# Loading the upper half of each w1 and w2 piece from ScalarE's queue

## The chip, the cores and the metric

The kernel runs on 1 core of one Trainium2 chip. The metric is the device time of one execution in microseconds (us); of several runs the median is given. Everything below about the hardware's behaviour is read from the profile of this kernel.

## The reference: what is computed

Two blocks, one after the other. The first is a delta-rule recurrence over 4 batches, 8 heads, 768 steps and 48 features a head; the second is a feed-forward block without a nonlinearity on the 3072 x 384 result.

```python
def _attn_ref(q, k, v, beta):                    # (4, 8, 768, 48)
    k_n = k / (np.linalg.norm(k, axis=-1, keepdims=True) + 1e-06)
    state = np.zeros((B, H, D, D), dtype=np.float32)
    for t in range(S):
        kt, vt, bt = (k_n[:, :, t], v[:, :, t], beta[:, :, t, None])
        y[:, :, t] = np.einsum('bhd,bhde->bhe', q[:, :, t], state)
        v_old = np.einsum('bhde,bhd->bhe', state, kt)
        state = state + bt[:, :, :, None] * np.einsum('bhd,bhe->bhde', kt, vt - v_old)
    return y

def _moe_ref(x, w1, w2, w3, w_out):              # x 3072x384, w1 w2 384x1024,
    a = x @ w1                                   # w3 1024x1024, w_out 1024x384
    b = x @ w2
    h = a * b @ w3
    return (h @ w_out).astype(np.float32)
```

q, k, v and beta come as 32-bit floats. The four weights come as 64-bit floats: a division by a numpy square root makes them so.

## The kernel before, in words

**The recurrence in chunks.** The 768 steps are cut into 12 chunks of 64. For each chunk the kernel makes score matrices of the keys (`scores`, L359), inverts the unit triangular matrices on VectorE, two chunks at a time and 32 x 32 blocks at a time (`inverse`, L422; its two long lines are L442 and L449), goes through DRAM to bring the blocks into another layout (`to_blocks` L410 writes Ud, L428 reads Ub, L457 writes Vd, `from_blocks` L463 reads TT and T), completes the inverse with small matmuls (`corner`, L480; products L502, copies L518 and L529), and carries the state along (`chain`, L547, matmuls L555). `outputs` (L623, matmuls L656) writes the chunk's result transposed into xT: eight ScalarE copies (L677), then six small DMAs inside SBUF (L688).

**The feed-forward block.** w3 and w_out are multiplied beforehand (`fold`, L768, matmuls L771 and copies L778, after the transposes L762 and copies L765 of w3), since nothing stands between them. Then, for every two chunks, `ab` (L784) makes (x w1) and (x w2): three matmuls over the 384 rows for each block of 128 columns (L791), a ScalarE copy of the first product (L803), and a VectorE multiplication by the second (L807). GpSimd makes sums of these slabs (L860) and `o` (L865, matmuls L888) and `result` (L915) the output.

**The 64-bit weights.** A weight is loaded as pairs of 32-bit words and converted in the kernel. `load_pair` (L701) loads one piece into one of three `raw` buffers in turn, 1 MB each; `convert` (L711) makes half of a piece: two ScalarE operations (L717, L720), a shift on VectorE (L722), a sum on GpSimd (L724). There are 18 pieces: 4 of w_out, 8 of w3, 3 of w1 and 3 of w2. A piece of w_out or w3 is one DMA over 128 partitions. A piece of w1 or w2 (`load_w12`, L741) is 128 rows of the weight in the order in which xT holds the features, and takes four DMAs: 48 rows to partitions 0 to 47, 16 rows to 48 to 63, 48 rows to 64 to 111, 16 rows to 112 to 127. Each row is 8 KB. The last two are called the upper half here. w_out's converted pieces lie in the buffer of w2, so w2's conversion waits until the folds have read them.

**The order.** No scheduler chooses the order: `ORDER` (L39) is a list of step names, and each name advances one generator by one step. P names are loads of pieces (P12 to P17 those of w1 and w2, in the order P13, P12, P14, P15, P17, P16), C names conversions, k, q, v and p the loads of keys, queries and values, a and b the steps of `ab`. `in_text_order` (L161) then fixes the order on each engine as written, so every engine works through its own list strictly in order. SyncE (SP) issues nearly all DMAs; ScalarE issues only those of the first chunk of k and q (`act.dma_start` at L980 and L991). An instruction that issues a DMA first waits for its buffer (here: until GpSimd's L724 has read the piece three back) and for its semaphore: the DMAs share eight of these, called lanes below, and the lane's last DMA must have landed. A waiting DMA instruction holds up what stands behind it in its engine's list.

Of the kernel before, what the change touches and what calls it, by code (L numbers as in the profile page):

```python
# [90 lines left out]
def kernel(  # L91
# [15 lines left out]
    C = 64  # L107
# [32 lines left out]
    def in_turn(pool, shape, tag, n, name, dt=FP32):  # L140

        i = turns.get(tag, -1)
        while True:
            i = turns[tag] = (i + 1) % n
            if (tag, i) not in held:
                return pool.tile(shape, dt, tag=f"{tag}{i}", name=name, bufs=1)
# [14 lines left out]
    def in_text_order():  # L161
# [7 lines left out]
    pe, dve, act, pool, sync = nc.tensor, nc.vector, nc.scalar, nc.gpsimd, nc.sync  # L169
# [7 lines left out]
        out=strict[:], in_=strict[:], pattern=[[1, P]], compare_op=ALU.is_gt,  # L177
# [523 lines left out]
    def load_pair(i, n, srcs):  # L701

        raw = raws[i] = in_turn(ffn, [P, 2, CW, 2], "raw", 3, "raw", U32)
        for rows, src in srcs:
            to = raw[rows, :, 0:n].rearrange("p b n w -> p b (n w)")
            if n == CW:
                to = to.rearrange("p b n -> p (b n)")
            sync.dma_start(out=to, in_=src)
        yield

    def convert(i, hf, n, dst):  # L711
# [21 lines left out]
    def load_wo(j):  # L733
        src = moe_w_out[2 * j * P : (2 * j + 2) * P, :].bitcast(U32)
        return load_pair(j, DM, [(slice(0, P), src.rearrange("(b p) n -> p b n", b=2))])

    def load_w3(jc):
        src = moe_w3[jc * P : (jc + 1) * P, :].bitcast(U32)
        return load_pair(KF // 2 + jc, CW, [(slice(0, P), src)])

    def load_w12(i, src, m):  # L741
        srcs = []
        for e in range(2):
            a, b = D * (NP * e + m), D * (NP * e + NP - 1) + 16 * m
            srcs.append((slice(C * e, C * e + D), src[a : a + D, :].bitcast(U32)))
            srcs.append((slice(C * e + D, C * e + C), src[b : b + 16, :].bitcast(U32)))
        return load_pair(i, CW, srcs)
# [317 lines left out]
```

## Time and profile before

| | |
|---|---|
| median of 3 runs | 602.34 us (601.66 to 604.63) |
| the profiled execution | 601.93 us |
| its span in the profile | 600.2 us |
| mean granted TensorE clock | 0.98 |
| busy: PE, DVE, ACT, POOL | 90%, 55%, 27%, 29% |
| chain that ended last, PE's share | 80% |
| DMA queue of SP | 54.52 MB, 46.4% of 16 engines |
| DMA queue of ACT | 0.79 MB, 0.9% |
| queue of instructions | 1.08 MB, 0.8% |

How to read it: PE is TensorE's matmuls and PEld its weight loads, DVE is VectorE, ACT ScalarE, POOL GpSimd, SP SyncE; a q behind the name (SPq, ACTq) is the engine's sequencer, which issues DMAs and isn't counted as busy. A row of a timeline has the start in us, the length in us, engine, line, operation, tile written and tiles read with their shapes, a count, and in brackets how long the engine had been idle and what ended that. "issue" there means that the engine waited for nothing that the profile shows. A row of the chain of waits has start, length, and what the time went to. The times of a DMA are its issue; how long it took to land is given by the view of its tile.

The six pieces in question, from SP's timeline and the landings (us):

| load | issued | landed |
|---|---|---|
| 1: P13, w1 m=1 | 74.07 to 75.39 | 78.9 to 82.6 |
| 2: P12, w1 m=0 | 93.86 to 96.30 | 100.1 to 104.1 |
| 3: P14, w1 m=2 | 96.82 to 98.16 | 107.4 to 110.6 |
| 4: P15, w2 m=0 | 118.12 to 120.54 | 123.9 to 127.8 |
| 5: P17, w2 m=2 | 127.95 to 130.90 | 133.5 to 137.0 |
| 6: P16, w2 m=1 | 140.01 to 141.51 | 145.0 to 148.9 |

### The profile page before, as it was taken

The page shows a single profiled execution, that of the slowest core. Times are in us where ns is not written, and L with a number is a line of the kernel's source. Part 1 is how long each engine was busy: PE and PEld are TensorE (multiplying, and loading weights), DVE is VectorE, ACT ScalarE, POOL GpSimd, SP SyncE. Part 2 cuts the span into 40 slices and gives each one's busy share as a digit, 9 for nine tenths or more (in the row PEclk, how much of TensorE's full clock was granted, in tenths as well). Part 3 has the DMA queues.
Part 4 walks back from the last instruction along what each step waited for, and adds up shares of the span by engine and source line. Part 5 has one row for each costly group of instructions (what it writes and reads, how often), then busy time and mean ns, then how long its engine had stood idle before and what let it go on. Part 6 is the DMA issues. An engine that isn't in the chain of part 4 may idle for free.

```text
span 600.2 us, 19394 instructions
## 1 busy us (share of the span) xinstructions
PE 542.4 (90%) x8444; PEld 378.7 (63%) x8444; DVE 329.7 (55%) x788; ACT 164.2 (27%) x345; POOL 173.6 (29%) x222
## 2 busy tenths in 40 slices
PE   2378994889899999999999899999999999999997
PEld 2364663658678884558854569645588446884477
DVE  2457763457786379665696644975545963211012
ACT  3486653734312211131211312012310111320100
POOL 6364433230535700207203016021071001500051
PEclk9988996899999999999999989999999999999999
DMA  8959887596953356525546352463253021010001
GB/s 225 219 135 276 233 163 128 82 176 96 164 80 55 56 123 108 98 42 84 103 78 127 50 81 73 82 114 65 40 86 94 14 59 32 5 54 13 1 0 53
DMA packets 204404, 56.54 MB, mean 94 GB/s; under 512 B 193344, under 2 KB 199488, under 8 KB 202528
## 3 DMA queue, kind: packets, MB, share of 16 engines
q1 hardware_dynamic: 200128, 54.52, 46.4%
q10 hardware_dynamic: 4192, 0.79, 0.9%
q8 instruction: 66, 1.08, 0.8%
q14 instruction: 18, 0.15, 0.1%
HBM read 43.09 MB, written 11.01 MB: 90 GB/s over the span
## 4 chain that ended last, share of the span: by engine, by line
PE 80%; DMA 6%; issue 4%; DVE 4%; ACT 4%; SPq 1%; POOL 0%; ACTq 0%; DVEq 0%
PE ps_f L791 39%; PE ps_f L888 18%; PE ps_w L555 5%; PE ps_f L771 5%; PE ps_w L656 4%; DMA raw<-in_moe_w_dram 3%; PE ps_w L502 3%; PE ps_w L369 2%; PE ps_w L375 2%; DMA ktok<-in_k_dram 2%; DVE ps_w L449 1%; DVE tb L442 1%; DMA Vd<-Vb 1%; ACT raw L720 1%; PE ps_w L888 1%
## 5 line engine op out<-in xcount | busy, mean ns | idle before, releaser
L791 PE MATMUL ps_f<-xT,w2s 128*128 128x512 f32 (+1 forms) x336 | 134.2, 544 | 3.0 <-POOL w2s L724 2.8
L860 POOL TENSOR_TENSOR ab<-ab 128x256 f32<-128x256 f32 x96 | 66.8, 728 | 223.5 <-DVE ab L807 190.0
L791 PE MATMUL ps_f<-xT,w1s 128*128 128x512 f32 (+1 forms) x336 | 128.2, 532 | 0.3 <-issue 0.3
L791 PEld LDWEIGHTS ps_f<-xT,w2s 128*128 128x128 f32 x336 | 62.5, 191 | 57.9 <-issue 50.9
L791 PEld LDWEIGHTS ps_f<-xT,w1s 128*128 128x128 f32 x336 | 63.3, 190 | 55.8 <-issue 51.7
L803 ACT COPY ab<-ps_f 128x512 f32<-128x512 f32 (+1 forms) x56 | 27.9, 527 | 185.6 <-PE ps_f L791 185.6
L888 PE MATMUL ps_f<-w,ab 128*128 128x192 f32 x376 | 66.3, 330 | 0.0
L807 DVE TENSOR_TENSOR ab<-ab,ps_f 128x512 f32<-128x512 f32 (+1 forms) x56 | 32.9, 604 | 59.1 <-PE ps_f L791 58.5
L888 PEld LDWEIGHTS ps_f<-w,ab 128*128 128x128 f32 x376 | 61.2, 190 | 3.9 <-issue 2.7
L442 DVE TENSOR_TENSOR tb<-Vb,Ub 128x31 f32<-128x31 f32 (+15 forms) x124 | 43.9, 354 | 16.4 <-DMA Ub<-Ud 13.0
L771 PE MATMUL ps_f<-w2s,w3T 128*128 128x384 f32 x128 | 45.4, 507 | 4.9 <-ACT w3T L765 3.5
L888 PE MATMUL ps_f<-room,ab 128*128 128x192 f32 x272 | 48.0, 330 | 0.8 <-DVE room L919 0.8
L449 DVE TENSOR_TENSOR Vb<-Vb,tb 128x31 f32<-128x31 f32 (+15 forms) x124 | 44.6, 360 | 4.3
L888 PEld LDWEIGHTS ps_f<-room,ab 128*128 128x128 f32 x272 | 44.1, 190 | 1.6 <-issue 1.1
L677 ACT COPY xT<-ps_w 48x256 f32<-48x256 f32 x96 | 30.5, 366 | 49.1 <-PE ps_w L656 48.6
L272 POOL TENSOR_TENSOR sq<-ktok 128x384 f32<-128x384 f32 x24 | 20.2, 852 | 75.7 <-DVE tb L442 39.1
L381 DVE TENSOR_TENSOR U<-ps_w,wt 128x512 f32<-128x512 f32 x24 | 16.5, 689 | 42.6 <-PE ps_w L375 42.5
L771 PEld LDWEIGHTS ps_f<-w2s,w3T 128*128 128x128 f32 x128 | 24.2, 195 | 21.5 <-ACT w3T L765 4.0
L375 PE MATMUL ps_w<-KQ 48*64 48x64 f32 x768 | 29.4, 227 | 6.3 <-issue 4.7
L724 POOL TENSOR_TENSOR w<-w,raw 128x512 uint32<-128x512 uint32 x16 | 20.7, 1298 | 33.1 <-DVE w L722 15.7
L375 PEld LDWEIGHTS ps_w<-KQ 48*64 48x64 f32 x768 | 26.1, 140 | 5.6 <-issue 3.9
L541 POOL TENSOR_TENSOR vtok<-vtok,n 128x384 f32<-128x384 f32 x24 | 19.8, 838 | 33.3 <-DMA vtok<-in_v_dram 33.3
(104 smaller groups left out, 644.7 us busy)
## 6 DMA issues: line engine op xcount, KB each, us to landing
raw<-in_moe_w_dram SPq DMA_DIRECT2D x8, 1024.0 KB, 8.1
vtok<-in_v_dram SPq DMA_DIRECT2D x24, 192.0 KB, 4.5
raw<-in_moe_w_dram SPq DMA_DIRECT2D x12, 384.0 KB, 6.7
out_dram<-osb SPq DMA_DIRECT2D x46, 96.0 KB, 2.7
ktok<-in_k_dram SPq DMA_DIRECT2D x44, 96.0 KB, 3.5
raw<-in_moe_w_out_dram SPq DMA_DIRECT2D x4, 768.0 KB, 5.0
Ud<-U SPq DMA_DIRECT2D x48, 64.0 KB, 2.3
Ub<-Ud SPq DMA_DIRECT2D x6, 512.0 KB, 3.9
```

The lines of the kernel that those rows point to most:

```text
L375: pe.matmul(ps[half(z ^ j), 1, n + C * j : n + C * j + C], lhsT=x[:, 0, :], rhs=x[:, j, :], start=True, stop=True,)
L442: dve.tensor_tensor(out=tv, in0=V[:, 0 : s + 1, s : s + 1].to_broadcast([P, s + 1, n]), in1=U[:, s, s + 1 : BS].unsqueeze(1).to_broadcast( ...
L449: dve.tensor_tensor(out=o, in0=o, in1=tv, op=ALU.subtract)
L555: pe.matmul(out(ps, r, h, z), lhsT=lhs(r, h, z), rhs=rhs(r, h, z), start=True, stop=True,)
L656: i = pe.matmul(region(h, z, r), lhsT=lhs, rhs=rhs, start=part[n] not in part[:n], stop=part[n] not in part[n + 1 :],)
L677: act.copy(out=xT[f, p:NP:2, b : b + NR, cc, :].rearrange("p a r t -> p r a t"), in_=pyv[f, z, b : b + NR],)
L771: pe.matmul(ps[:, 0:DM], lhsT=w3Ts[jc, kc // 4][:, kc % 4 * P : kc % 4 * P + P], rhs=wo[:, kc], start=(kc == 0), stop=(kc == KF - 1),)
L791: pe.matmul(ps[:].rearrange("p b c t -> p b (c t)"), lhsT=w[:, m, js], rhs=x[:, m, :, c0:c1].rearrange("p b c t -> p b (c t)"), start=(m = ...
L803: act.copy(out=t, in_=ps)
L807: dve.tensor_tensor(out=t, in0=t, in1=ps, op=ALU.mult)
L860: pool.tensor_tensor(out=o_, in0=x_, in1=y_, op=op)
L888: pe.matmul(ps[b][:, b, :], lhsT=abs_[u, HF * f + i][:, t0 : t0 + P], rhs=ws_[w][:, i], start=first and i == 0 and (b == 0 or n == "F"), s ...
```

## The change

In `load_pair` the DMA of a row range that begins at partition 64 or above (C is 64) is issued by ScalarE, every other one by SyncE as before. Only `load_w12` hands over such ranges, two of four for each piece, so 12 DMAs of 3 MB in all move. The buffers, the bytes, the converted results and ORDER stay as they are; in ScalarE's list a moved DMA stands where its step stands in ORDER. The lanes are dealt out anew, so that some DMAs of SP now share a lane with one of ScalarE, and the reverse.

```diff
         raw = raws[i] = in_turn(ffn, [P, 2, CW, 2], "raw", 3, "raw", U32)
         for rows, src in srcs:
+            dma = act.dma_start if rows.start >= C else sync.dma_start
             to = raw[rows, :, 0:n].rearrange("p b n w -> p b (n w)")
             if n == CW:
                 to = to.rearrange("p b n -> p (b n)")
-            sync.dma_start(out=to, in_=src)
+            dma(out=to, in_=src)
         yield
```

The function that hands over the ranges:

```python
def load_w12(i, src, m):
    srcs = []
    for e in range(2):
        a, b = D * (NP * e + m), D * (NP * e + NP - 1) + 16 * m
        srcs.append((slice(C * e, C * e + D), src[a : a + D, :].bitcast(U32)))
        srcs.append((slice(C * e + D, C * e + C), src[b : b + 16, :].bitcast(U32)))
    return load_pair(i, CW, srcs)
```

## The prediction

> **What bounds the kernel now.** I read the page first, then the chain of work that ended last, then PE's waits and its timeline, and at the places found there the timelines of SP and ACT and the DMA view. From the page:
>
> ```profile
> PE 542.4 (90%) x8444; PEld 378.7 (63%) x8444; DVE 329.7 (55%) x788; ACT 164.2 (27%) x345; POOL 173.6 (29%) x222
> ...
> q8 instruction: 66, 1.08, 0.8%
> ...
> raw<-in_moe_w_dram SPq DMA_DIRECT2D x12, 384.0 KB, 6.7
> ```
>
> PE is busy for 90% of the span. The windows put its idle time early: between 220 and 600 us it idles 9.8 of 380 us, between 75 and 180 us it idles 18.8 of 105. The six loads that the change touches are issued at 74.07, 93.86 (two), 118.12, 127.95 and 140.01 us, all in that early part, so only what reaches PE before about 180 us counts; behind that PE passes on whatever delay or lead it has. PE's timeline there:
>
> ```profile
> 96.28 0.47 PE L375 MATMUL ps_w<-KQ 48*64 48x64 f32 x2 [2.19 <-issue]
> ...
> 105.59 0.33 PE L502 MATMUL ps_w<-T,U 33*33 33x32 f32 x4 [6.15 <-issue]
> ...
> 113.21 0.91 PE L771 MATMUL ps_f<-w2s,w3T 128*128 128x384 f32 x2 [0.74 <-issue]
> ...
> 130.90 0.98 PE L656 MATMUL ps_w<-PT,X 64*48 64x64 f32 x50 [2.22 <-issue]
> ...
> 157.90 0.70 PE L791 MATMUL ps_f<-xT,w2s 128*128 128x256 f32 x2 [2.29 <-POOL w2s L724]
> 159.14 6.09 PE L791 MATMUL ps_f<-xT,w2s 128*128 128x256 f32 x27 [0.54 <-POOL w2s L724]
> ```
>
> Two things stop PE. The last two rows are the sixth load, told below. The "issue" rows wait for no semaphore. The page has 66 packets of 16 KB on the instruction queue, and PE has 16,888 matmuls and weight loads: 256 instructions a packet. In the DMA view one such packet comes between 102 and 104 us, with PE back at 105.59; one between 110 and 112, PE back at 113.21; one between 128 and 130, PE back at 130.90. So PE waits there for its own code. Where no bulk load is in flight (112 to 118 us) the packet follows about 1 us after PE entered the block before it (113.21, packet at 114.4); with the second and third load in flight it took 6.2 us (PE entered at 96.28, packet at 102.5), with the fourth 6.9 us (121.16, 128.1). Each time it came when the pieces issued before the request had landed. **Code comes late behind bulk loads**; that is the larger cost, and the change moves such loads.
>
> The sixth load (w2, m = 1), in the chain:
>
> ```profile
> 141.51 7.39 DMA raw<-in_moe_w_dram
> 148.92 0.68 ACT w2s L717
> 149.63 0.43 DVE w2s L722
> ```
>
> The last piece, an upper half, lands at 148.90; ACT converts at 148.92; DVE stood 2.60 us for it; POOL's sum and PE's first w2 products follow at 157.90 and 159.14. The first lower piece landed 4.9 us after its issue, the last upper one 7.4.
>
> **What the change moves.** Of 24 pieces, 12 (six of 48 rows, six of 16) leave SP and go to ACT, at the place in ACT's program where the load stands. SP saves 12 x 0.42 us (median of its row) = 5.0 us of issuing. ACT gains 12 x 0.42 to 0.69 us (0.69 is its own X load at 10.84) = 5.0 to 8.3 us of its sequencer. ACT is 27% busy. What matters is when ACT reaches the instruction, and what stands behind it.
>
> ACT's sequencer runs ahead of its engine:
>
> ```profile
> 9.77 0.65 ACT L717 ACTIVATE w<-raw 128x512 f32<-128x512 f32 x1
> 10.20 0.60 ACTq L215 DMA_DIRECT2D X<-in_q_dram  x1
> 10.32 0.66 ACT L720 ACTIVATE raw<-raw 128x512 uint32<-128x512 uint32 x1
> ```
>
> The X load stands behind L720 in the program and is issued before it begins. The sequencer's semaphore records of L717 at 110.24 stand five instructions ahead of the one that starts at 110.22. So I let an upper half issue when five instructions before it are still to run. Its bounds: no run-ahead (up to 2.4 us later) and no limit.
>
> **Load 1 (w1, m = 1).** SP 74.07; ACT reaches it at about 75.4, beside the 74.92 of now. It is converted at 88.38 and landed by 82.6; 5.8 us cover it. Vd, queued behind it (78.31, landing 84.45), may land 2 us sooner, but PE is busy with L771 and L762 until 88.2: 0, bounds -0.8 to 0.
>
> **Loads 2 and 3 (w1, m = 0 and 2).** SP now issues 1 MB instead of 2 MB from 93.86. The code packet of 102.5 waited for the first 896 KB; the same 896 KB, now two lower halves, are ahead of it. So the 6.15 us stay: 0, bounds -2.5 (as if only the first 512 KB, landing 100.8, were ahead) to 0. The packet of 110.67 waited for the rest, which is gone: -1.2 (112.0 to 113.21, the weight load's gap, of which the PE row has 0.74).
> ACT reaches the uppers at about 110.3, in the fifth of eight xT copies (108.93 to 111.5), four issues until 112. By load 1's row (4.8 to 7.2 us) they land from 115 to 119, where ACT now converts at 112.66. Behind them in ACT stand five conversions, the w3T copy and L529, which now starts at 119.54: 115.8 for load 2, 119 for load 3, then 4.6 us, so L529 ends at about 124.7. L555 at 123.94 reads it: +0.8. The next code packets are asked for at about 112 and 118.5, beside the upper halves and load 4: +1 to +2.6 for the first, up to +5.3 with the second, partly the same wait as L529's. I take **+2.0 less 1.2 = +0.8** at 121 us, bounds -1.2 to +5.3.
>
> **Load 4 (w2, m = 0).** SP's half waits for a semaphore lane whose last user is ACT's piece: 119 instead of 118.12. The conversion (127.92) waits for PE's L771 in any case: 0. With both halves in flight together it is over sooner, and the 2.22 us at 130.90 may go: already in the bounds.
>
> **Load 5 (w2, m = 2).** The second piece shares a lane with an xT copy inside SBUF (issued 134.64, landing 137.2), so ACT's sequencer stands until about 138 and the ab copy of 137.1 comes 0.5 to 1 us later. PE has four banks to go on: 0, bounds 0 to +1.
>
> **Load 6.** ACT reaches it when its 140.39 copies start: issue 141.7 to 142.2, now 141.05 and 141.51. SP's perm pieces no longer wait for the upper half (one issue now stands 3.49 us, from 144.96), so ktok is issued at 147 to 148 instead of 150.14, and POOL's L724 of 156.56 moves up to 2.6 us; the conversion is then held by ACT's own order (147.7), 1.2 us before 148.92. PE's 2.83 us behind L724 are the most to win; the second L724 pair (161.30) follows DVE, which gains only 1.2: **-2.3**, bounds -2.8 to +3 (upper as late as now's 7.4 us from 144.5).
>
> Two rates bear on this: a load over 128 partitions ran at 403 GB/s (window 60 to 64), the halves one after another at 169 (96 to 108) and 180 (142 to 146), with the DMA engines fully busy in all three. [...]
>
> **Sum.** 0 + 0.8 + 0 + 0 - 2.3 = -1.5 us. The profiled execution took 601.93 (span 600.2), 0.4 below the median of 602.34: 600.4 there, **600.8** as a median.
>
> **Rivals.**
> *Faster, 597.5.* Code is held less: the 6.15 us shrink by 1.7 (packet when the first 512 KB landed), -1.2 and the 2.22 us stay won, ACT's queue doesn't hold packets (at 14 to 16 us small X packets of ACT's queue alternated with SP's bulk), and load 6 gives 2.3, less some overlap: about -4.8. Against: every packet beside bulk came late.
> *Slower, 606.5.* ACT is late at loads 2 and 3. The point: the last upper landing L; L + 5.8 must not exceed 123.9, so each us behind 118.1 is one of PE. With 12.5 us from issue, load 3's row of now, L is 122.7 to 124.5 and PE loses 4.6 or more; code asked for meanwhile waits too (+5.3 alone). If load 6 gives back 1, +4.2. For: ACT's program there is dense and these uppers start some 14 us later than now (95.84 to 98.16). Against: the 12.5 us were behind 2 MB.
> *It does nothing:* the order of the built program has SP 12 pieces less and ACT 12 more, the compute order of the engines the same, so it does what it says.
>
> **How the numbers follow.** The near-cancelling forecast 0.43 (its own range 598.5 to 604.5), faster 0.27, slower 0.30. 0.5%, about what a measurement of this kernel can tell from no change, is 3.0 us: 599.3 to 605.4. Faster: 0.26 of its rival and 0.05 of the forecast, 0.31; slower 0.30; within 0.39. The range reaches into both rivals: 597.0 to 607.5.
>
> **What would show it.** Right: PE's 6.15 us stay, the 0.74 goes, ACT stands 3 to 5 us before L717 near 113 to 119, and the gap before 157.90 shrinks. Wrong: uppers of loads 2 and 3 issued well behind 110 us; a code gap over 3 us between 113 and 127; load 6's upper landing behind 150; or the 6.15 us gone.

## The result, and the profile after

The changed kernel takes 604.13 us (median of 20 runs, 598.47 to 608.18) beside 601.5 us for the kernel before (20 runs, 597.16 to 606.66). The ratio is 1.0051, 95% interval [1.0028, 1.0075]: slower by 0.5%, some 3 us, where 1.5 us less was forecast. The profiled execution took 602.13 us, with a span of 600.3 us and a granted clock of 0.965 (before 600.2 us and 0.98). The ratios leave out runs over 1.5% above the fastest of their kernel (5 of the 12 of e12_late_on_sp, at most 2 of any other kernel in the table below), and the profile of e4_load6, which is of such a run, isn't used. The two profiled executions took the same time to 0.2 us: their traces show which waits moved, and only the 20 runs of each kernel show that time was lost.

The page first: the busy row, and the two data queues with packets, MB and share of 16 engines.

```profile
PE 547.3 (91%) x8444; PEld 382.5 (64%) x8444; DVE 328.1 (55%) x788; ACT 164.3 (27%) x345; POOL 173.4 (29%) x222
...
q1 hardware_dynamic: 199552, 51.38, 43.6%
q10 hardware_dynamic: 4768, 3.93, 3.9%
```

3.14 MB have gone from q1 to q10, as the diff says. PE does the same instructions as before and is busy 4.9 us longer, at the lower mean clock (0.965 against 0.98). PE's timeline, with what ended each idle time:

```profile
87.99 0.76 PE L502 MATMUL ps_w<-T,U 33*33 33x32 f32 x64 [1.26 <-DVE T L485]
...
94.45 0.47 PE L375 MATMUL ps_w<-KQ 48*64 48x64 f32 x2 [1.30 <-issue]
...
101.84 0.33 PE L502 MATMUL ps_w<-T,U 33*33 33x32 f32 x4 [4.21 <-issue]
...
121.56 0.31 PE L555 MATMUL ps_w<-R,TT 64*64 64x48 f32 x2 [0.53 <-ACT TT L529]
122.17 1.14 PE L555 MATMUL ps_w<-R,TT 64*64 64x48 f32 x62 [0.30 <-ACT TT L529]
...
130.80 4.55 PE L792 MATMUL ps_f<-xT,w1s 128*128 128x256 f32 x20 [1.09 <-issue]
...
152.60 2.86 PE L792 MATMUL ps_f<-xT,w1s 128*128 128x256 f32 x12 [1.95 <-ACT ab L804]
...
156.72 0.70 PE L792 MATMUL ps_f<-xT,w2s 128*128 128x256 f32 x2 [0.84 <-POOL w2s L725]
157.97 2.21 PE L792 MATMUL ps_f<-xT,w2s 128*128 128x256 f32 x9 [0.55 <-POOL w2s L725]
```

Against the rows of before: the 6.15 us for code are 4.21, the 0.74 and the 2.22 are gone (1.09 at a later place instead), the wait for w2's sum went from 2.83 to 1.39. New are 1.26 for T, 0.83 for L529 and 1.95 for an ab copy. This execution also ran 2.6 us ahead of the first profile before any of the six loads is issued, so times are compared below by their distance from a neighbour, not by where they stand.

### The profile page after: what moved, and what is told of

Read it like the earlier page. It is cut to its first block, busy times and chain, and to the rows that moved or that the text cites. A ratio compares the mean times of both kernels' runs of the same rounds, so it can differ in the third digit from the quotient of the medians.

```text
span 600.3 us, 19395 instructions
## 1 busy us (share of the span) xinstructions
PE 547.3 (91%) x8444; PEld 382.5 (64%) x8444; DVE 328.1 (55%) x788; ACT 164.3 (27%) x345; POOL 173.4 (29%) x222
## 4 chain that ended last, share of the span: by engine, by line
PE 80%; DMA 7%; ACT 4%; issue 3%; DVE 2%; SPq 1%; ACTq 1%; POOL 0%; POOLq 0%; DVEq 0%
PE ps_f L792 40%; PE ps_f L889 19%; PE ps_w L555 5%; PE ps_w L656 4%; PE ps_f L772 4%; PE ps_w L502 3%; DMA raw<-in_moe_w_dram 2%; DMA ktok<-in_k_dram 2%; PE ps_w L369 2%; PE ps_w L375 2%; ACT KQ L349 1%; DMA xT<-xT 1%; PE ps_f L339 1%; ACT raw L721 1%; ACT xT L677 1%
## 5 line engine op out<-in xcount | busy, mean ns | idle before, releaser
L792 PE MATMUL ps_f<-xT,w2s 128*128 128x512 f32 (+1 forms) x336 | 132.5, 539 | 2.0 <-POOL w2s L725 1.4
L442 DVE TENSOR_TENSOR tb<-Vb,Ub 128x31 f32<-128x31 f32 (+15 forms) x124 | 43.3, 349 | 16.3 <-DMA Ub<-Ud 12.8
L772 PE MATMUL ps_f<-w2s,w3T 128*128 128x384 f32 x128 | 48.0, 531 | 3.6 <-ACT w3T L766 3.6
L889 PE MATMUL ps_f<-room,ab 128*128 128x192 f32 x272 | 49.4, 336 | 0.8 <-DVE room L920 0.8
L889 PEld LDWEIGHTS ps_f<-room,ab 128*128 128x128 f32 x272 | 45.4, 194 | 1.6 <-issue 1.1
L272 POOL TENSOR_TENSOR sq<-ktok 128x384 f32<-128x384 f32 x24 | 19.8, 835 | 77.8 <-DVE Vb L449 29.5
L772 PEld LDWEIGHTS ps_f<-w2s,w3T 128*128 128x128 f32 x128 | 25.7, 207 | 21.0 <-ACT w3T L766 4.1
L725 POOL TENSOR_TENSOR w<-w,raw 128x512 uint32<-128x512 uint32 x16 | 20.9, 1309 | 31.5 <-DVE w L723 16.9
L369 PE MATMUL ps_w<-KQ 48*64 48x128 f32 x384 | 28.4, 289 | 1.1 <-issue 0.9
```

The lines of the kernel that those rows point to most:

```text
L369: pe.matmul(ps[half(z), 0, n : n + 128], lhsT=x[:, 0, :], rhs=x.rearrange("p j t -> p (j t)"), start=True, stop=True,)
L442: dve.tensor_tensor(out=tv, in0=V[:, 0 : s + 1, s : s + 1].to_broadcast([P, s + 1, n]), in1=U[:, s, s + 1 : BS].unsqueeze(1).to_broadcast( ...
L772: pe.matmul(ps[:, 0:DM], lhsT=w3Ts[jc, kc // 4][:, kc % 4 * P : kc % 4 * P + P], rhs=wo[:, kc], start=(kc == 0), stop=(kc == KF - 1),)
L792: pe.matmul(ps[:].rearrange("p b c t -> p b (c t)"), lhsT=w[:, m, js], rhs=x[:, m, :, c0:c1].rearrange("p b c t -> p b (c t)"), start=(m = ...
L889: pe.matmul(ps[b][:, b, :], lhsT=abs_[u, HF * f + i][:, t0 : t0 + P], rhs=ws_[w][:, i], start=first and i == 0 and (b == 0 or n == "F"), s ...
```

## The experiments

All kernels compute the whole result. Each was timed in 12 runs (the last two in 6) between runs of the kernel before on the same chip, and profiled once. Two theories were on the table. **Late issue**: the halves go out when ACT's list lets them, later than SP did, and what waits for them is late. **Two queues**: a half costs by flying on the second queue, wherever it stands.

| kernel | uppers on ACT | ratio to before |
|---|---|---|
| the change | all six | 1.0051 [1.0028, 1.0075] |
| e9_again | all six | 1.0027 [0.9996, 1.0058] |
| e1_load1 | 1 | 0.9987 [0.9957, 1.0017] |
| e2_loads23 | 2, 3 | 1.0026 [0.9990, 1.0061] |
| e3_loads45 | 4, 5 | 1.0008 [0.9978, 1.0037] |
| e4_load6 | 6 | 1.0035 [1.0000, 1.0069] |
| e5_early | all, five earlier in ACT's list | 1.0024 [0.9992, 1.0057] |
| e6_load6_early | 6, earlier | 0.9987 [0.9958, 1.0016] |
| e7_all_but6 | 1 to 5 | 0.9993 [0.9957, 1.0029] |
| e8_loads23_early | 2, 3, earlier | 1.0047 [1.0020, 1.0073] |
| e10_6early | all, 6 earlier | 1.0012 [0.9978, 1.0047] |
| e11_all_but23 | 1, 4, 5, 6 | 1.0020 [0.9982, 1.0057] |
| e12_late_on_sp | none, 6 late on SP | 0.9975 [0.9937, 1.0012] |
| e13_before | none (the kernel before) | 0.9978 [0.9945, 1.0010] |
| e14_loads2345 | 2 to 5 | 1.0009 [0.9976, 1.0042] |
| e15_6later | 6, later still | 1.0084 [1.0053, 1.0115] |
| e16_4and6early | 4, and 6 earlier | 1.0032 [1.0005, 1.0059] |
| e17_6mid | 6, earlier, other lanes | 1.0149 [1.0101, 1.0197] |
| e18_4and6mid | 4, and 6 earlier, other lanes | 1.0080 [1.0048, 1.0113] |

0.001 is 0.6 us. The change repeated (e9_again) gave 1.0027, and the unchanged kernel as a kernel of its own 0.9978, so a ratio within 0.003 of 1 says little by itself.

### One load at a time

```diff
-            dma = act.dma_start if rows.start >= C else sync.dma_start
+            dma = act.dma_start if rows.start >= C and i in (13,) else sync.dma_start
```

(13,) is load 1; (12, 14) are loads 2 and 3, (15, 17) loads 4 and 5, (16,) load 6.

> Only the upper half of load 1 (w1, m=1) goes over ACT's queue, the other five loads stay on SP's. Late-issue theory: ACT hands the two pieces out only when the fold copy L779 ahead of them starts, some 4 to 6 us later than SP did; Vd lands earlier, but X, TT and T that follow on SP then fly beside the late half, and PE's first corner product (L502) stands up to 1.5 us for T: +0.5 to +1.5 us. Contention theory (each half on a second queue costs the same): +0.5 us. Clock theory (the whole program gets a lower granted clock, no step of the load matters): 0, within 0.5 us.

> Only the upper halves of loads 2 and 3 (w1, m=0 and 2) go over ACT's queue. Late-issue theory: the halves go out some 12 us later, in the run of xT copies, and L529 ends later by about 0.5 us, but PE's code packets behind the bulk come 1.5 to 2 us earlier at the first place and up to 2 us earlier at the second: -3 to 0 us. Contention theory: +1 us. Clock theory: 0, within 0.5 us.

> Only the upper halves of loads 4 and 5 (w2, m=0 and 2) go over ACT's queue. Late-issue theory: load 4 goes out at its old time (0), load 5 by 4 us later and with it the conversions of its piece and the ab copies behind them: 0 to +1.5 us. Contention theory: +1 us. Clock theory: 0, within 0.5 us.

> Only the upper half of load 6 (w2, m=1) goes over ACT's queue. Late-issue theory: it goes out only after a conversion that itself waits, 4 to 5 us later than SP did, lands 2 to 3 us later, ACT stands about 4 us before the conversion with four ab copies behind it, PE runs out of banks and stands about 2 us for them: +1.5 to +3.5 us, the largest share of the whole change. Contention theory: +0.5 us. Clock theory: 0, within 0.5 us.

Measured: 0.9987, 1.0026, 1.0008 and 1.0035. Together that is +3.4 us, about the whole of the change, with load 6 the largest as late issue has it. But each interval is 3 to 4 us wide and none is clear of 1, and load 1 alone read faster where late issue had +0.5 to +1.5 us, so the sum settles nothing. The next kernels take load 6 out, bring it early and make it later.

### Load 6: out, early, later

In e7_all_but6 load 6 stays on SP (`i != 16`). For the others the upper half is a step of its own, U16, and is put elsewhere in ORDER; only ACT's list changes by that, and the lanes are dealt out anew.

```diff
             parts[f"P{i}"] = lambda i=i, src=src, m=m, es=(0,) if early else (0, 1): load_w12(i, src, m, es)
+            parts[f"U{i}"] = lambda i=i, src=src, m=m: load_w12(i, src, m, (1,))
...
-c1 b6 V1 b6 y1 a05 b3
+c1 b6 V1 U16 b6 y1 a05 b3
```

That is the early place (e6, e10, e16). e15 puts U16 right ahead of C32, the conversion that needs it.

> The changed kernel with load 6's upper half back on SP's queue. Late-issue theory, with the single parts adding up: about 2 us less than the changed kernel, +0.5 to +1.5 us against before; PE's wait for the ab copies near 150 us is gone. Two-queue theory, each half megabyte the same: 5/6 of the whole, +2.5 us.

> Only load 6's upper half on ACT's queue, but ahead of the third ab copy in ACT's list, so that it goes out no later than SP's lower half. Late-issue theory: the +2 us of the load 6 kernel are gone and ACT no longer stands 4 us before the conversion; if both halves in flight overlap, the landing comes up to 3 us earlier than before: -2.5 to +0.5 us. Two-queue theory: still about +2 us.

> The changed kernel, all six uppers on ACT, with one difference: load 6's stand ahead of the third ab copy in ACT's list. Late-issue theory for load 6: the time falls back by 2 to 3.5 us, to -1 to +1 us against before, and PE doesn't stand for ab copies behind load 6's conversion. Two-queue theory: still about +3 us.

> Only load 6's upper half on ACT's queue, and two ab copies later still, right ahead of the conversion that needs it: its issue moves from about 4 us behind SP's old one to 6 or 7. Late-issue theory for load 6: the wait before the conversion and PE's stand grow by about 2 us: +3.5 to +5 us. If the +2 us of the load 6 kernel have another cause (the second queue, chance): +2 us again, or 0.

Measured: without load 6 0.9993, early 0.9987 alone and 1.0012 with the other five, later still 1.0084. The dose answers: +2.1 us late, +5.0 us later, and the interval of e15 lies clear above those of e6, e7 and e10. (With the other five, early and late hardly separate: 1.0012 against 1.0027 and 1.0051.) The traces agree at this place. The time from a fixed product of w1 (PE at 141.85 us in before) to the fixed w2 product behind the last of load 6's waits (159.14) is, in us:

| load 6's upper half | profiles |
|---|---|
| on SP, as before | before 17.3, e13 15.1, e1 15.7, e2 15.6, e3 17.5, e7 17.0, e8 15.7, e14 16.1: mean 16.3 |
| late on ACT | the change 18.1, e9 18.0, e11 18.4 |
| later still on ACT | e15 20.2 |
| early on ACT | e5 15.6, e6 14.4, e10 15.7, e16 15.2 |

Late costs 1.9 us there, later 4.0, early saves 1.0. Two profiles of the unchanged kernel lie 2.2 us apart, so what counts is that the late ones lie above all eight with the half on SP. PE's waits in this stretch are 3.3, 3.3 and 2.3 us in the late ones, 3.1 in e15, 0.6 to 3.0 (mean 1.8) on SP and at most 0.2 in the early ones. The rest is work at half clock: 3.4 us of it in e11, 5.8 in e15, 2.4 to 3.4 in e5, e10 and e16. For load 6 alone late issue holds, and the rival falls: e6 has the half on ACT's queue and loses nothing. The timeline of the changed kernel shows how late (ACT, with a row of SP):

```profile
143.34 0.67 ACT L718 ACTIVATE w2s<-raw 128x512 f32<-128x512 f32 x1
...
143.45 0.80 ACTq L709 DMA_DIRECT2D raw<-in_moe_w_dram  x2
...
149.01 2.70 SPq L204 DMA_DIRECT2D ktok<-in_k_dram  x4
149.96 0.67 ACT L718 ACTIVATE w2s<-raw 128x512 f32<-128x512 f32 x1 [4.07 <-DMA raw<-in_moe_w_dram]
...
152.19 1.17 ACT L804 COPY ab<-ps_f 128x256 f32<-128x256 f32 x4
```

SP issued the lower half at 135.03 and 135.60. ACT's list reached the upper one at 143.45, once the conversion ahead of it had started; it landed at 148.94 and 149.80. ACT stood 4.07 us, four ab copies stood behind it, and PE, out of banks, for 1.95. PE waited so for an ab copy at this place in all five of these traces with a late half (changed kernel 1.95, e9 2.42, e11 1.94, e15 3.06, and e12 below 2.26 us), and in none with the half on SP in its old place.

### The same lateness on SP, and the lanes

```diff
-C34 P16 V1 a06 b0 b7
+C34 P16 p4 U16 V1 a06 b0 b7
```

In e12_late_on_sp U16 is issued by SP, behind the eight perm pieces, which move up for it.

> No DMA on ACT's queue: all pieces on SP as before, but load 6's upper half stands behind the eight perm pieces in SP's list instead of ahead of them, so that it goes out near 145 us. Late-issue theory for load 6: the queue doesn't matter, only when the half lands, 2 to 3 us later than before: +1 to +3 us. Two-queue theory: 0, within 0.7 us.

Measured: 0.9975 (by the medians of all runs 600.40 beside 599.72 us, 1.0011), and 16.6 us from the w1 to the w2 product, within the range of the half in its old place. So no loss shows, and no gain that both numbers share; the interval overlaps that of load 6 late on ACT (1.0035), so the two are not clearly apart by time. Issued at 143.30, landed at 149.89, ACT stood 4.40 us and PE 2.26 for the ab copy. So the late landing alone, as I had put it, doesn't seem to be what costs. What differs is on SP and POOL (e12's timeline):

```profile
144.34 2.70 SPq L204 DMA_DIRECT2D ktok<-in_k_dram  x4
...
152.27 0.83 POOL L272 TENSOR_TENSOR sq<-ktok 128x384 f32<-128x384 f32 x1 [16.14 <-DMA ktok<-in_k_dram]
...
152.55 2.86 PE L794 MATMUL ps_f<-xT,w1s 128*128 128x256 f32 x12 [2.26 <-ACT ab L806]
...
153.06 2.54 POOL L727 TENSOR_TENSOR w2s<-w2s,raw 128x512 uint32<-128x512 uint32 x2
```

ktok goes out at 144.34, before the upper half has landed. POOL's square of it (L272), which stands ahead of w2's sum in POOL's list, begins while PE still waits for ACT, and the sum is made at 153.06 to 155.60, while PE works on w1: the wait for w2 is gone. In the changed kernel ktok went at 149.01, 0.07 us after ACT's 48 rows had landed at 148.94, with which it shares a lane. SP's waits from 140 to 152 us name it:

```profile
SPq L204 <- DMA raw<-in_moe_w_dram: 5.3, 1, 5.3
...
SPq L204 <- PE ps_f L792: 0.4, 1, 0.4
```

ktok's issue (L204) stood 5.3 us for a raw load; in e15 it stood 6.9, and in e12 SP has no such wait there. From ktok the changed kernel's chain (start, length, what) leads to w2's product:

```profile
139.59 9.78 PE ps_f L792 x44
149.37 0.30 SPq L204
...
149.72 0.64 SPq L204
...
150.40 0.63 SPq L204
...
151.07 3.37 DMA ktok<-in_k_dram
...
155.39 2.54 POOL w2s L725 x2
...
157.97 6.09 PE ps_f L792 x27
```

The chain's first row is PE's because of the 0.4 us above; that issue took 0.66 us, hardly more than the two behind it, so the lane had held ktok until then. The price of load 6 is then two waits of PE in a row, one through ACT and its ab copies, one through lane, SP, ktok and POOL; late on SP, the second is hidden under the first. The second is 1.39 us in the changed kernel, 0.89 in e9 and 0.32 in e11, and none in e15, where PE was held 3.06 us and then worked at half clock while POOL made the sum. That the lane, and not something else that moved with it, makes the difference is read from such hand-overs, not tried by itself.

e6_load6_early shows the lane at another place. In its chain PE's wait near 143 us runs back over an xT copy to ACT's half:

```profile
136.57 4.91 DMA raw<-in_moe_w_dram
141.48 0.02 issue
141.50 2.01 DMA xT<-xT
143.51 0.14 issue
143.64 2.48 PE ps_f L794 x10
```

So an early half takes the wait for w2 away (0.17 us left) and here puts one for xT in its place (1.55). With load 4 as well (e16) that wait is 4.7 us, and there bulk in the way is part of it: the copy that PE waited for was issued at 135.31 and landed 7.2 us later, where before the six took 1.9 to 3.7. The last two kernels move U16 behind b6 and y1, so that the xT copies get other lanes.

> Two parts that the traces show as gains, put together: load 4's upper half on ACT's queue where the changed kernel has it (PE's code stall near 128 us shrinks), and load 6's ahead of the third ab copy (no wait before w2's first product). Stall theory: the two gains add to 2 to 4 us of PE's stalls, -3 to -1 us against before. If stalls saved near 100 to 160 us are given back at half clock: -0.5 to +0.5 us.

> Only load 6's upper half on ACT's queue, one ab copy later than in the early kernel, so that its two DMAs are dealt other lanes: the six xT copies on SP no longer share a lane with it, only the lower half of load 6 does. Lane theory (the early kernels lost near 140 us what they won at w2's conversion, because an xT copy on SP waited for the lane of ACT's half): PE's wait for xT near 140 us is gone, the wait for w2 stays short, -2.5 to -0.5 us against before. If the early kernels lost it to bulk ahead of the xT copies and not to the lane: PE still waits 1.5 us or more near 140 us, -0.5 to +1 us.

> Load 4's upper half on ACT's queue where the changed kernel has it, and load 6's one ab copy later than in the early kernels, with lanes that no xT copy shares. Lane theory: the 4.7 us that PE stood for xT in the kernel with loads 4 and 6 early are gone, and the time with it: -3.5 to -0.5 us against before. If not the lane: +1 to +2.5 us again.

Measured: 1.0032, 1.0149 and 1.0080; my expectations of a gain fell in all three. The wait for xT at this place is down to 0.80 and 1.07 us, as the lane theory has it. But the lane now goes to SP's own lower half, and the chain of e17 shows what stood behind that:

```profile
138.97 4.69 DMA raw<-in_moe_w_dram
...
143.72 0.32 SPq L711
...
150.72 0.66 SPq L204
...
153.47 3.46 DMA vtok<-in_v_dram
156.93 2.53 POOL w2s L727 x2
```

SP's lower half, eight perm pieces, ktok and vtok all come behind ACT's landing at 143.66, SP having stood 6.0 us for that lane, and PE waits 3.25 us for w2. (The chain goes over vtok; POOL's square of ktok ends at 156.97, with the start of w2's sum.) From the w1 to the w2 product it is 18.7 us in e17 and 18.9 in e18, 2.5 more than with the half on SP. That covers half of e18's 4.8 us; why e17 lost 8.9 by its ratio, with 6 runs, isn't settled.

### Loads 2 and 3, and all of them early

```diff
-K3 e1 e1 C23 t15
+K3 C23 U12 U14 e1 e1 t15
```

e8_loads23_early has this alone; C23, a conversion of another piece, moves up with it, so the kernel doesn't test the place of the halves by itself. e5_early has it and U13 before t9, U17 before y1 and U16 before b6. e11_all_but23 and e14_loads2345 choose the loads with `i` as above.

> Only the upper halves of loads 2 and 3 on ACT's queue, ahead of the L518 copies in ACT's list, so that they go out near 95 us beside SP's lower halves and not near 107 us. Late-issue theory: L529 and the conversions are no later than before: -1 to +0.5 us, against +1.6 us with the late place. Two-queue theory: +1 to +2 us as with the late place.

> All six upper halves on ACT's queue as in the changed kernel, but five of them (all but load 4) stand earlier in ACT's list, ahead of the instructions that wait for PE, where ACT arrives when SP issues the lower halves: load 1 ahead of the w3T copy before the two Vb copies, loads 2 and 3 ahead of the L518 copies that stand through PE's code stall, load 5 ahead of the xT copies, load 6 ahead of the third ab copy. Late-issue theory: what made the changed kernel slower is gone, landings are no later than in the kernel before, and the time is 3 us below the changed kernel's or more: -3 to +0.5 us against before. Two-queue theory (the second queue itself costs, by contention or by held code): still +2 to +4 us. PE's code stall near 100 us is 6 us again, since all of loads 2 and 3 are queued ahead of it.

> The changed kernel once more, beside the next three on one chip. Both theories: +3 us against before (+1.7 to +4.5), PE standing near 150 us for ACT's ab copies behind the late conversion of load 6. If the traces' half-clock stretch near 100 us decides the time of a single execution, this profile may show 10 to 24 us of it, whatever the kernel.

> The changed kernel with the uppers of loads 2 and 3 back on SP. If those two loads cost by being on a second queue (the kernels with loads 2 and 3 alone gave +1.6 and +2.8 us): 1.6 to 2.8 us less than the changed kernel, about +0.5 to +1.5 us. If only load 6's lateness costs: still +2 to +3.5 us.

> Uppers of loads 2 to 5 on ACT's queue, loads 1 and 6 on SP. Theory that the code packet behind load 4 decides: in the kernels with loads 2 and 3 alone PE stood 3.4 to 3.6 us near 128 us for the packet behind load 4; with load 4's halves on two queues it passes there, and the +1.6 to +2.8 us of those kernels are gone: -1 to +0.8 us. Theory that loads 2 and 3 cost by themselves: +1.5 to +3 us.

> The kernel before, unchanged, as a kernel of its own: what the comparison gives where nothing differs, and a second profile of it. Both theories: 0, within 1.5 us. Its profile shows whether the 13.6 us at half clock near 100 us and the 6.1 us code stall of the first profile come back or differ from execution to execution; if the half-clock stretch is set by where its free-running window falls, it may be 10 to 24 us here.

Measured: 1.0047, 1.0024, 1.0027, 1.0020, 1.0009 and 0.9978. Early or late, loads 2 and 3 alone read slower (late not clear of 1), so late issue doesn't explain them; together with others (e7, e10, e14) they read the same as before. My explanation for e14, the code packet behind load 4, doesn't stand: PE's 3.4 to 3.6 us near 128 us, which I had put down to these two kernels, are 3.59 in e13_before too. What loads 2 and 3 cost, and whether, stays open.

e8 answers another question, since both halves of both loads are in flight together there. Its window from 96 to 106 us, and the window of before from 98 to 108 (the last three columns are clock, DMA share and GB/s):

```profile
96.00:106.00 10.00, 3.18 (x128) 3.06 (x128) 2.64 (x5) 0.00 (x0) 1.28 (x1) 0.50 0.99 167
```

```profile
98.00:108.00 10.00, 3.85 (x132) 3.33 (x129) 1.43 (x4) 1.63 (x3) 1.28 (x1) 0.50 1.03 161
```

167 against 161 GB/s: two queues carried hardly more than one. From the first issue to the last landing the 2 MB took 14.7 us instead of 16.7. What let a piece over 128 partitions reach the 403 GB/s of the prediction, at the same share of the DMA engines (1.00), isn't settled by these runs.

### The clock

The half-clock stretch near 100 us, in windows of the kernel before and of the changed one:

```profile
core 0: us, PE busy (x) PEld busy (x) DVE busy (x) ACT busy (x) POOL busy (x), PEclk, DMA share, GB/s
95.70:109.30 13.60, 6.62 (x204) 5.91 (x208) 2.64 (x5) 2.91 (x7) 1.62 (x2) 0.50 1.01 160
```

```profile
90.40:110.80 20.40, 14.63 (x367) 12.05 (x359) 5.40 (x11) 9.37 (x20) 6.78 (x7) 0.50 0.67 108
```

PE worked 6.6 us at half clock before, 14.6 after. The clock moved in steps of 3.41 us or multiples (13.65 us here in before, 20.48 in the changed kernel). e15 shows the step at load 6:

```profile
147.80:151.20 3.40, 3.40 (x18) 2.99 (x17) 0.00 (x0) 0.01 (x1) 0.00 (x0) 1.00 0.78 154
151.20:154.60 3.40, 1.38 (x7) 0.87 (x5) 0.87 (x3) 1.60 (x3) 0.00 (x0) 1.00 0.17 33
154.60:158.00 3.40, 2.36 (x6) 1.90 (x7) 3.16 (x10) 1.80 (x6) 0.36 (x1) 0.51 0.88 161
158.00:161.40 3.40, 3.40 (x10) 2.65 (x9) 2.98 (x12) 0.24 (x1) 3.40 (x4) 0.50 1.23 174
161.40:164.80 3.40, 3.40 (x17) 3.01 (x16) 2.49 (x5) 2.51 (x6) 2.28 (x3) 0.99 0.80 107
```

Read PE's column and the clock: a window with 1.38 us of work is followed by half clock, a window of 2.36 doesn't end it, a full one does; and at half clock 10 matmuls fill the window that 17 or 18 fill otherwise. PE's wait of 3.06 us here has thus a second price in the windows behind it.

Over 19 profiles I took the time between two fixed instructions of PE (near 74 and 208 us) apart. It is 109 to 111 us, plus PE's waits, plus half of PE's busy time (weight loads included) at half clock; some of them:

| profile | time | waits | busy at half clock |
|---|---|---|---|
| before | 134.3 | 20.9 | 6.7 |
| e13_before | 134.1 | 19.1 | 10.4 |
| the change | 137.6 | 18.0 | 18.2 |
| e9_again | 137.0 | 18.7 | 15.3 |
| e12_late_on_sp | 134.0 | 18.6 | 11.7 |
| e11_all_but23 | 138.1 | 16.3 | 25.6 |
| e15_6later | 140.6 | 19.4 | 25.0 |

Over the 19, this time goes with the half-clock time in it (correlation 0.83) and not with the waits (0.08). In the changed kernel's two profiles PE waits less than in the two of before and is later all the same. How much of that is the change's doing the profiles can't say: the grid of windows stood at another place in every execution, and over whole runs the mean clock hardly differs (0.966 in the runs of the change and in those of e9, 0.966 to 0.967 in those of the kernel before beside the experiments). Only in e15 does it stand out: 0.959 over its 12 runs, 0.967 in the runs beside them.

## Why the prediction was wrong, point by point

**Load 6, -2.3 us: this step failed.** It had ACT issuing at 141.7 to 142.2, some 1.7 us behind SP's first lower piece, the half there by 147.7, when ACT's own order lets the conversion begin, and ktok at 147 to 148. Measured from SP's lower piece (135.03), ACT's issue came 8.4 us later and the last landing 14.8, where before it was 8.9. SP's piece itself went out earlier than before; measured from PE's w1 product (139.92 here, 141.85 before) the first upper piece was issued 4.3 us later than before and the last one landed 2.8 us later. Instead of -2.3 us, load 6 alone measured +2.1 (0.0 to +4.1). Two premises were wrong. The run-ahead of five instructions held only where none of the five waited. At loads 2 and 3 it held exactly (issue 106.54, with three xT copies and two conversion instructions still to run). At load 6 the list ahead had ab copies waiting for PE and a conversion, and the DMA went out with that conversion's start; at load 1, ACT's timeline of the changed kernel has the same:

```profile
77.42 0.48 ACT L779 COPY w<-ps_f 128x384 f32<-128x384 f32 x1 [1.73 <-PE ps_f L772]
77.43 0.84 ACTq L709 DMA_DIRECT2D raw<-in_moe_w_dram  x2
```

And the halves didn't fly together, nor would that have brought much: 167 GB/s in e8 with both in flight, 161 in before. The -2.3 us rest on the half being there by 147.7, which was the author's estimate; no run shows that gain, nor that landing for a half issued from this place: in the changed kernel ACT's two pieces landed at 148.94 and 149.80. That ktok shares a lane with ACT's half was left out of the step: it freed SP from its own late half and didn't see SP wait for ACT's. And there was less to win than the one profile showed: PE's wait for w2 was 2.83 us in it and 0.56 in e13_before, the same kernel.

**Load 1, 0.** Right in the time (0.9987), in part by luck, for it was late: issued 6 us behind SP's lower piece, not 1.3. X and TT then fly beside it (issued at 76.16 and 79.08, while the half landed at 85.98), and PE stood 0.9 to 1.3 us for T in all six traces that have it late; the stall for code near 100 us was 3.1 to 4.2 us in five of those six, and 4.8 to 7.5 in the others but for two (3.4 and 3.7). A wait that the term didn't have and a gain that it didn't have thus offset each other.

**Loads 2 and 3, +0.8.** Right in the mechanism: landing at 112.9 to 116.5, late conversions, L529, and PE waits 0.83 us for it (0.3 in e9 and nothing in e2, with these halves as late). The 6.15 us of code stay when only these loads move (5.86 in e2), and the 0.74 go. One reading behind the term was loose: the code packet of 102.5 set out 0.9 us before the third of the pieces that it was said to wait for had landed (103.44). The price of these two loads stays open, as told.

**Loads 4 and 5.** 0 and 0 to +1 are in line with 1.0008. The 2.22 us behind load 4's code packet go, as was held possible, but about half comes back some instructions later.

**The clock: missing from the sum.** The mean granted clock of 0.98 stood in the table of before, and the prediction counted waits alone. A wait saved near 100 us lies beside work at half clock (6.6 us of it in before, 14.6 in the changed kernel), and it needn't become time: the code stall there went from 6.15 to 4.21 us, and no time was won. Nor need PE be idle to be halved: of 50 full-clock windows in which it was busy for less than 57%, 40 were followed by half clock (next but one section).

**Rivals.** The slower one was priced at loads 2 and 3, from 118.1 us for the last landing; it came at 116.47 in a trace that runs 2.25 us early, so just at that point, with the 0.83 us that follow from it. The loss came from load 6, whose lateness was only the upper end of a bound (+3). Of the faster rival the saved waits came in the profile (the 6.15 us became 4.21, the 0.74 went, the 2.22 became 1.09), and PE's waits fell from 20.9 to 18.0 us; yet no time was won, since PE's work at half clock rose from 6.7 to 18.2 us. Signs that were to show the forecast right came as well (the 0.74 went, the wait at w2's first product fell from 2.29 to 0.84 us): they looked neither at PE's wait for ab copies nor at the clock.

## What to carry to other kernels

Here a DMA put into a compute engine's list went out when that list got there, load 6's half 8.4 us behind SP's, with ACT 27% busy: ask what the list waits for, not how busy the engine is. Where DMAs of several engines share semaphore lanes, a late bulk load on one of them can hold unrelated small transfers on another (ktok's issue stood 5.3 us for ACT's half), so follow the lane to who is released by the landing. Before moving transfers for parallelism look whether the DMA engines have room (here a share of 0.99 to 1.03, with one queue and with two), and count a saved wait as time only where PE's clock is full behind it (here 2.9 us less of waits came with 11.5 us more of work at half clock).

## What the runs showed of the hardware

The granted clock followed PE's busy share in windows of 3.41 us, taken here on the edges of the clock's own steps. The windows didn't start with the program: counted from the span's start, the edges lie 0.08 us past a multiple of 3.413 us in before and 1.62 us in the changed kernel. In 19 profiles, from 55 to 590 us: of 50 full-clock windows with PE busy for less than 57%, 40 were followed by half clock; of the 26 from there to 61%, 14; of 2,773 above 61%, one. Of 86 half-clock windows below 94%, 12 were followed by full clock; of 44 above, 43. So, as an estimate from these counts, a wait of 1.5 us that falls into one window, 44% of it, can halve the clock of the next, and one that straddles two may cost nothing more: before's 2.83 us at 155 to 159 us fell into two windows with PE busy for 57% and 61%, and neither was followed by half clock; e15's 3.06 us had two at half clock behind them.

The spread between runs of one kernel goes with it in part: in 34 runs of the kernel before, from 595.6 to 604.0 us, 0.01 less of mean clock went with 1.2 us more time (correlation -0.38). A single profile is one draw from that spread, and so was the one that the prediction was made from.
